# Four edits to an attention-plus-two-MLPs kernel: a weight's fetch behind stores, scores in shared banks, masks as two float32r parts, value means in place

## The chip, the cores and the metric

The kernel runs on one core of a Trainium2 chip. A run's time is the device time of one launch in microseconds (us). The time of a kernel is the median of its runs. TensorE is written PE here, VectorE DVE, ScalarE ACT, GpSimd POOL and SyncE SP; SP issues every transfer of this kernel.

## The reference

Three stages follow each other; all tensors are float32 except the six weight matrices, which are float64.

```python
# attention: batch 4, 8 heads, 768 tokens, head size 64; block 32, window 16
k_sum = k.reshape(B, H, nb, 32, D).max(axis=3)         # 24 block maxima of the keys
v_sum = v.reshape(B, H, nb, 32, D).mean(axis=3)        # 24 block means of the values
scores_l = where(|i - j| < 16, scale * q @ k.T, -1e9)  # local window
scores_s = scale * q @ k_sum.T + log(32)               # 24 summary columns
a = softmax(concat([scores_l, scores_s]))
x = a @ concat([v, v_sum])                             # 3072 tokens x 512
# first MLP, 512 -> 768 -> 512
h = maximum(maximum(x @ w1, x @ w2), x @ w3);  x = h @ w_out
# second MLP, 512 -> 2048 -> 512
h = x @ w_in;  out = (h * tanh(log1p(exp(h)))) @ w_out2
```

## The kernel before

**Number format.** A float32 matmul operand is written as a sum of two float32r parts, high and low, and a product is three float32r matmuls (high x high, high x low, low x high). A float32 operand can also be given to PE directly (`ident`, `mask`, the transposes).

**Attention** is done in 24 units of 128 tokens (6 for each batch). For unit `u`, `s2` multiplies queries with a window of 96 keys and 24 block maxima (`KX` = 120 columns) for 8 heads; the heads stand as 2 rows `r` of 4. The first three units (`u < PEMASK`) let PE add the mask: a matmul of the identity with the mask starts each bank (L435), and the scores are added to it. From the fourth unit on DVE adds the mask while it moves the scores out of PSUM (L452). DVE then finds the negative maximum (L455), ACT takes the exponentials (L459), `s2b` normalises, `s3` transposes the probabilities in two halves (`ptp`, L479, moved out as `pT` by ACT at L481), and `s4` multiplies with the values (`xp`, L493) and splits the result into high and low parts (`xh`, `xl`) for the first MLP. `q_prep` and `k_prep` transpose queries and keys (`tp`, L344); `k_prep` also takes the block maxima (`ksum`, L358) and stores transposed keys through the single buffer `kst` (L355, L360). `v_prep` takes block means of the values of batch 1 (`vp`, L298) and stores them through `vc`, which shares the buffer `kst` (L308 to L310).

**Weights.** A weight chunk is 128 rows x 512 float64 values (512 KB). `run_job` moves four chunks one step each through fetch (L159, three buffers `words`), absolute value on ACT (L169), five or six DVE instructions that make float32 out of float64 (L177 to L190) and a last step. For the first 24 chunks, those of the first MLP, the last step (`into`) leaves high and low parts in SBUF; the first 14 of them use PE to add up (`wp`, L232 to L234). For the 32 chunks of the second MLP (`later_jobs`, `keep`) the last step splits the chunk (L254, L255) and stores both parts to DRAM (`w2d`, L256 and L257), to be loaded later by `load_b`. A step is taken at each of the first units, and from token block 2 of the first MLP on once in three groups.

**First MLP.** Eight blocks of 384 tokens, each with 22 groups: 18 products of `gemm1` (`hp`, 12 matmuls, L584 to L586) and 4 of `gemm2` (`yp`, 18 matmuls, L618 to L620). ACT or DVE drains each result (L592, L596, L600, L622). Five steps of each attention unit are emitted between these groups. `y` goes to DRAM (L623).

**Second MLP.** Eight blocks of 384 tokens x 16 steps: `g3` (`up`, L677 to L679), an activation on ACT and DVE (L688 to L718), and `g4` into three accumulators (`acc`, L732 to L734).

[...] Before the change: pool `gps` has three one-bank buffers for `hp`, `yp`, `wp` and part of `up`; `aps` has three for `tp`, `vp`, `ptp` and `xp`; `asc` has one buffer of two banks for the scores `sc`. In the second MLP `aps` and `asc` are given back, and `ups` (two banks) and three accumulators take their place.

**Order.** The code above gives an order, and a scheduler that plans with its own model of the engines moves instructions within what data, buffers and `tc.issue_after` (this instruction comes after that one) allow. On the chip each engine then takes its instructions in that fixed order, so an instruction that waits holds up those behind it on its engine; that is also true of SP's transfers.

Of the kernel before, what the change touches and what calls it, by code (L numbers as in the profile page):

```python
# [10 lines left out]
F32 = mybir.dt.float32  # L11
# [3 lines left out]
ALU = mybir.AluOpType  # L15
# [38 lines left out]
def tile_kernel(ctx, tc, q, k, v, w1, w2, w3, w_out, w_in2, w_out2, out):  # L54
# [27 lines left out]
    dpool = ctx.enter_context(tc.tile_pool(name="dpool", bufs=1, space=DRAM))  # L82
    gps = ctx.enter_context(tc.tile_pool(name="gps", bufs=3, space=PSUM))

# [41 lines left out]
    g2 = agem.enter_context(tc.tile_pool(name="g2", bufs=1))  # L126

    att = ExitStack()
    ap1 = att.enter_context(tc.tile_pool(name="ap1", bufs=1, side="right"))
    ap2 = att.enter_context(tc.tile_pool(name="ap2", bufs=2, side="right"))  # L130
    ap3 = att.enter_context(tc.tile_pool(name="ap3", bufs=3, side="right"))
    stage = att.enter_context(tc.tile_pool(name="stage", bufs=WB, side="right"))
    aps = att.enter_context(tc.tile_pool(name="aps", bufs=3, space=PSUM))
    asc = att.enter_context(tc.tile_pool(name="asc", bufs=1, space=PSUM))

# [20 lines left out]
    def fetch(src):  # L156
        words = stage.tile([P, 1024], U32, name="words", tag="words")
        o, x = src(words)
        last["words"] = nc.sync.dma_start(out=o, in_=x)  # L159
        return words  # L160
# [90 lines left out]
    def keep(f, i):  # L251
        def done(w, _):
            h = stage.tile([P, 512], F32R, name="wr", tag="wr", bufs=AB)
            nc.scalar.copy(h, w)  # L254
            nc.vector.tensor_tensor(out=w, in0=w, in1=h.bitcast(F32), op=ALU.subtract)  # L255
            nc.sync.dma_start(out=w2d[f][:, 2 * i], in_=h.bitcast(F32))  # L256
            nc.sync.dma_start(out=w2d[f][:, 2 * i + 1], in_=w)  # L257

        return done
# [43 lines left out]
    def v_prep(b, g):  # L303

        t = nat.pop(("v", b, g))
        vp = aps.tile([P, H, D], F32, name="vp", tag="a")
        mean_v(vp[0:NS].rearrange("p h d -> p (h d)"), t, 0, NS, True, True)
        vc = ap1.tile([P, H, D], F32, name="vc", tag="kst")[0:NS]  # L308
        nc.scalar.copy(vc, vp[0:NS])
        nc.sync.dma_start(out=vsd[b][:, g * NS : (g + 1) * NS, :].rearrange("h n d -> n h d"), in_=vc)  # L310
# [59 lines left out]
    def q_prep(b, g):  # L370
        tp = turn("q", b, g)
        nc.scalar.mul(qT[(b * NG + g) % RQ], tp, scale)
# [43 lines left out]
    def bank(name):  # L416
        return aps.tile([P, NP, P], F32, name=name, tag="a")
# [9 lines left out]
    def s2(u):  # L427

        t = u % NG
        mask = masks["first" if t == 0 else "last" if t == NG - 1 else "mid"]  # L430
        sc = asc.tile([P, 2, 512], F32, name="sc", tag="sc")
        add = u >= PEMASK
        if not add:
            for r in range(2):
                nc.tensor.matmul(  # L435
                    sc[:, r, 0 : NP * KX], lhsT=ident, rhs=mask.unsqueeze(1).to_broadcast([P, NP, KX]),
                    start=True, stop=False,
                )
        for p in range(NP):
            for e in reversed(range(GT)):  # L440
                for r in range(2):
                    d = slice(r * D, (r + 1) * D)
                    c = slice(e * QT, (e + 1) * QT)
                    nc.tensor.matmul(
                        sc[c, r, p * KX : (p + 1) * KX], lhsT=qT[u % RQ][d, p, c], rhs=kT[(GT * u + e) % RK][d, p],
                        start=add, stop=add or p == NP - 1,
                    )
        s = ap2.tile([P, H, KX], F32, name="s", tag="s", bufs=SB)
        src = sc[:, :, 0 : NP * KX].rearrange("q r (p x) -> q r p x", p=NP)
        if add:  # L450
            wide = mask.unsqueeze(1).unsqueeze(1).to_broadcast([P, 2, NP, KX])
            nc.vector.tensor_tensor(out=heads(s), in0=src, in1=wide, op=ALU.add)  # L452
            src = heads(s)
        nm = ap2.tile([P, 2, NP], F32, name="nm", tag="nm")
        nc.vector.tensor_reduce(out=nm, in_=src, axis=AX.X, op=ALU.max, negate=True)  # L455
        sm = ap2.tile([P, H], F32, name="esum", tag="esum")
        for h in range(H):
            r, p = divmod(h, NP)
            nc.scalar.activation(  # L459
                out=s[:, h], in_=src[:, r, p], func=AF.Exp, bias=nm[:, r, p : p + 1], accum_out=sm[:, h : h + 1]  # L460
            )
        rs = ap2.tile([P, H, 1], F32, name="rs", tag="rs")
        att_t[u] = (s, sm, rs)
# [169 lines left out]
    def open_second():  # L633
# [5 lines left out]
        sec["t1"] = pool("bt1", 1)  # L639
        sec["up"] = sec["stack"].enter_context(tc.tile_pool(name="ups", bufs=2, space=PSUM))  # L640
        sec["ps"] = sec["stack"].enter_context(tc.tile_pool(name="bps", bufs=1, space=PSUM))
# [28 lines left out]
    def g3(i, f):  # L670
        xh, xl = x2hl[i]
        w = wb[f]
        more = (i * NF2 + f) % 5 > 2
        pt = (sec["up"] if more else gps).tile([P, 512], F32, name="up", tag="g")
        for c in range(KC):
# [85 lines left out]
    for T in range(RK):  # L761
        load_k(T)
    q_prep(0, 0)
    load_v(0)
    load_v(1)
    s2(0)
    run_job()
    s2b(0)
# [116 lines left out]
```

## Time and profile before

| | |
|---|---|
| median of 3 runs | 1132.24 us (1132.17 to 1132.39) |
| the profiled execution | 1133.17 us, of which the trace's span is 1131.4 us |
| busy in the span | PE 1098.0, DVE 812.4, ACT 549.6, POOL 75.8 us |
| mean granted PE clock | 0.994 of full speed |
| moved by DMA | 125.49 MB |
| second MLP | from about 540 us to the end |

A busy PE in this profile is not a PE at its peak: matmuls are pipelined, and their ends are modelled. In a row of the windows view the numbers are the stretch, its length, then for each engine busy us and instructions, the granted PE clock, the share of the DMA engines' time that was used and GB/s. In a row of the waits view they are who waited, for whom, us in total, times and the longest.

### The profile page before, as it was taken

The numbers are of one execution on the slowest core, as the hardware profiler recorded it, in microseconds if no ns is written. First come the engines' busy times: TensorE is split into PE (matmuls) and PEld (weight loads), VectorE is DVE, ScalarE is ACT, GpSimd is POOL, SyncE is SP. The second block draws the span as 40 slices with busy tenths as digits, with TensorE's granted clock in tenths as the row PEclk, the third lists the DMA queues.
The fourth block names the chain that finished last, engine by engine and source line by source line (L and its number), as shares of the span: only waits on it lengthen the run. The fifth ranks groups of instructions, "written<-read, shape, count | busy, mean of one in ns | idle before, by whom it ended". The sixth has DMA issues, their size and how long they took to land.

```text
span 1131.4 us, 18637 instructions
## 1 busy us (share of the span) xinstructions
PE 1098.0 (97%) x7004; PEld 987.8 (87%) x7004; DVE 812.4 (72%) x1595; ACT 549.6 (49%) x1336; POOL 75.8 (7%) x132
## 2 busy tenths in 40 slices
PE   6888999999999899999999999999999999999998
PEld 3557889999898899999999998989889898999887
DVE  5678934287887789852238887787878888787775
ACT  4676535345544554632125554545545455454543
POOL 3000012211113110100000000000000000000000
PEclk9999999999999899999999999999999999999999
DMA  9897745466887857521557010100001010000000
GB/s 234 217 253 201 174 126 135 125 172 197 225 215 221 228 172 201 159 68 52 179 189 288 15 57 1 55 2 23 35 1 56 1 29 29 14 29 1 29 1 28
DMA packets 179730, 125.49 MB, mean 111 GB/s; under 512 B 125048, under 2 KB 161400, under 8 KB 177592
## 3 DMA queue, kind: packets, MB, share of 16 engines
q1 hardware_dynamic: 179640, 124.30, 39.0%
q8 instruction: 55, 0.90, 0.3%
q14 instruction: 35, 0.29, 0.1%
HBM read 88.05 MB, written 35.05 MB: 109 GB/s over the span
## 4 chain that ended last, share of the span: by engine, by line
PE 77%; DVE 10%; ACT 5%; DMA 4%; issue 3%; POOL 1%; SPq 0%; ACTq 0%; POOLq 0%; DVEq 0%
PE up L679 8%; PE up L677 8%; PE acc L732 8%; PE up L678 8%; PE acc L733 8%; PE acc L734 8%; PE hp L584 6%; PE hp L586 6%; PE hp L585 6%; ACT s L459 3%; PE yp L618 2%; PE yp L620 2%; PE yp L619 2%; PE xp L493 1%; DVE words L182 1%
## 5 line engine op out<-in xcount | busy, mean ns | idle before, releaser
L695 ACT ACTIVATE r<-n,two 128x384 f32<-128x384 f32 x128 | 78.9, 616 | 153.9 <-DVE n L692 153.9
L584 PE MATMUL hp<-xh,a 128*128 128x384 f32 x384 | 133.9, 349 | 6.3 <-ACT m L592 3.4
L586 PE MATMUL hp<-xh,a 128*128 128x384 f32 x384 | 129.3, 337 | 0.0
L585 PE MATMUL hp<-xl,a 128*128 128x384 f32 x384 | 129.3, 337 | 0.0
L718 DVE TENSOR_TENSOR gl<-g,gh 128x384 fp32r<-128x384 f32 x128 | 71.3, 557 | 64.2 <-ACT gh L717 63.8
L688 ACT ACTIVATE e<-up 128x384 f32<-128x384 f32 x128 | 63.0, 492 | 98.8 <-PE up L679 97.9
L584 PEld LDWEIGHTS hp<-xh,a 128*128 128x128 f32 x384 | 72.4, 188 | 11.1 <-ACT m L592 4.3
L459 ACT ACTIVATE s<-s,nm 128x120 f32<-128x120 f32 x168 | 64.0, 383 | 29.5 <-DVE nm L455 29.5
L705 DVE TENSOR_TENSOR p<-up,r 128x384 f32<-128x384 f32 x128 | 70.6, 552 | 5.5 <-ACT r L696 5.5
L585 PEld LDWEIGHTS hp<-xl,a 128*128 128x128 f32 x384 | 72.5, 189 | 0.8 <-issue 0.5
L586 PEld LDWEIGHTS hp<-xh,a 128*128 128x128 f32 x384 | 72.4, 189 | 0.1
L690 DVE TENSOR_SCALAR ep<-e 128x384 f32<-128x384 f32 x128 | 45.9, 358 | 35.8 <-ACT e L688 35.3
L710 DVE SCALAR_TENSOR_TENSOR g<-u,n 128x384 f32<-128x384 f32 x128 | 70.9, 554 | 0.8
L708 DVE SCALAR_TENSOR_TENSOR u<-u,p 128x384 f32<-128x384 f32 x128 | 70.7, 552 | 0.4
L692 DVE SCALAR_TENSOR_TENSOR n<-e,ep 128x384 f32<-128x384 f32 x128 | 70.7, 552 | 0.3
L707 DVE SCALAR_TENSOR_TENSOR u<-n,r 128x384 f32<-128x384 f32 x128 | 70.3, 549 | 0.0
L717 ACT CAST gh<-g 128x384 fp32r<-128x384 f32 x128 | 64.3, 502 | 9.4 <-DVE g L710 9.4
L584 PE MATMUL hp<-xh,b 128*128 128x384 f32 x192 | 67.8, 353 | 0.3 <-ACT y L622 0.3
L696 ACT ACTIVATE r<-r 128x384 f32<-128x384 f32 x128 | 67.1, 524 | 1.0
L618 PE MATMUL yp<-hh,c 128*128 128x384 f32 x192 | 65.6, 344 | 0.1
L677 PE MATMUL up<-x2h,a 128*128 128x384 f32 x192 | 64.5, 336 | 0.0
L678 PE MATMUL up<-x2l,a 128*128 128x384 f32 x192 | 64.5, 336 | 0.0
(167 smaller groups left out, 2886.0 us busy)
## 6 DMA issues: line engine op xcount, KB each, us to landing
words<-in_moe_w_out SPq DMA_DIRECT2D x22, 512.0 KB, 4.7
words<-in_moe_w SPq DMA_DIRECT2D x18, 512.0 KB, 5.3
words<-in_moe_w_in SPq DMA_DIRECT2D x16, 512.0 KB, 3.9
w2d<-wr SPq DMA_DIRECT2D x32, 256.0 KB, 4.6
w2d<-wa SPq DMA_DIRECT2D x32, 256.0 KB, 5.2
kT<-kTd SPq DMA_DIRECT2D x35, 192.0 KB, 5.1
vr<-in_v SPq DMA_DIRECT2D x35, 192.0 KB, 3.6
nat<-in_q SPq DMA_DIRECT2D x24, 256.0 KB, 4.3
```

Of the source, the lines that this page charges most:

```text
L459: nc.scalar.activation(out=s[:, h], in_=src[:, r, p], func=AF.Exp, bias=nm[:, r, p : p + 1], accum_out=sm[:, h : h + 1])
L584: nc.tensor.matmul(pt[:, :n], lhsT=wh, rhs=xh[:, c, :n], start=(c == 0), stop=False)
L585: nc.tensor.matmul(pt[:, :n], lhsT=wh, rhs=xl[:, c, :n], start=False, stop=False)
L586: nc.tensor.matmul(pt[:, :n], lhsT=wl, rhs=xh[:, c, :n], start=False, stop=(c == KC - 1))
L618: nc.tensor.matmul(pt[:, :n], lhsT=wh, rhs=hh[:, :n], start=(f == 0), stop=False)
L677: nc.tensor.matmul(pt[:, :N2], lhsT=wh, rhs=xh[:, c], start=(c == 0), stop=False)
L678: nc.tensor.matmul(pt[:, :N2], lhsT=wh, rhs=xl[:, c], start=False, stop=False)
L679: nc.tensor.matmul(pt[:, :N2], lhsT=wl, rhs=xh[:, c], start=False, stop=(c == KC - 1))
L695: nc.scalar.activation(out=r, in_=d["n"], func=AF.Ln, bias=two[:, 0:1])
L732: nc.tensor.matmul(o, lhsT=gh[:, c], rhs=w[:, 2], start=(f == 0), stop=False)
L733: nc.tensor.matmul(o, lhsT=gh[:, c], rhs=w[:, 3], start=False, stop=False)
L734: nc.tensor.matmul(o, lhsT=gl[:, c], rhs=w[:, 2], start=False, stop=(f == NF2 - 1))
```

## The change

1. `fetch` issues a weight's fetch after the last store of the split weights (`last["store"]`), once there has been one. Nothing changes for the first 24 chunks.
2. The two-bank pool `asc` is gone. A unit's scores are two one-bank tiles, one for each row of heads, out of `aps`, which has four banks now. The free bank goes to `gps`, which has four. DVE's mask addition, and for the first three units its maximum, is done a row at a time. `ups` is gone; `up` lives in the four banks of `gps`.
3. The masks of the first three units are split into two float32r parts at the start (in the space of tiles `hh5`, `hl5`); PE adds them by two float32r matmuls a row in place of one float32 matmul.
4. `v_prep` writes the means over the tile that held the values (`t`), not to `kst`.

In the program's first lines `run_job` and `s2(0)` also come ahead of the loads of the first values.

```diff
-    gps = ctx.enter_context(tc.tile_pool(name="gps", bufs=3, space=PSUM))
+    gps = ctx.enter_context(tc.tile_pool(name="gps", bufs=4, space=PSUM))
...
+    split_masks = {}
+    for kind, tag in (("first", "hh5"), ("mid", "hl5")):
+        both = gx.tile([P, MAXT * QT], F32R, name=f"both_{kind}", tag=tag)
+        h, l = both[:, 0:KX], both[:, KX : 2 * KX]
+        nc.vector.tensor_copy(h, masks[kind])
+        nc.vector.tensor_tensor(out=l, in0=masks[kind], in1=h.bitcast(F32), op=ALU.subtract)
+        split_masks[kind] = h, l
...
-    aps = att.enter_context(tc.tile_pool(name="aps", bufs=3, space=PSUM))
-    asc = att.enter_context(tc.tile_pool(name="asc", bufs=1, space=PSUM))
+    aps = att.enter_context(tc.tile_pool(name="aps", bufs=4, space=PSUM))
...
-        last["words"] = nc.sync.dma_start(out=o, in_=x)
+        with tc.issue_after(last["store"].ins) if "store" in last else nullcontext():
+            last["words"] = nc.sync.dma_start(out=o, in_=x)
...
-            nc.sync.dma_start(out=w2d[f][:, 2 * i + 1], in_=w)
+            last["store"] = nc.sync.dma_start(out=w2d[f][:, 2 * i + 1], in_=w)
...
-        vc = ap1.tile([P, H, D], F32, name="vc", tag="kst")[0:NS]
+        vc = t[0:NS]
...
-        sc = asc.tile([P, 2, 512], F32, name="sc", tag="sc")
+        sc = [bank("sc") for r in range(2)]
...
-                nc.tensor.matmul(
-                    sc[:, r, 0 : NP * KX], lhsT=ident, rhs=mask.unsqueeze(1).to_broadcast([P, NP, KX]),
-                    start=True, stop=False,
-                )
+                for j, m in enumerate(split_masks[kind]):
+                    nc.tensor.matmul(
+                        sc[r][:, :, 0:KX], lhsT=one_r, rhs=m.unsqueeze(1).to_broadcast([P, NP, KX]),
+                        start=(j == 0), stop=False,
+                    )
...
-            wide = mask.unsqueeze(1).unsqueeze(1).to_broadcast([P, 2, NP, KX])
-            nc.vector.tensor_tensor(out=heads(s), in0=src, in1=wide, op=ALU.add)
+            for r in range(2):
+                wide = mask.unsqueeze(1).to_broadcast([P, NP, KX])
+                nc.vector.tensor_tensor(out=heads(s)[:, r], in0=src[r], in1=wide, op=ALU.add)
...
-        sec["up"] = sec["stack"].enter_context(tc.tile_pool(name="ups", bufs=2, space=PSUM))
...
-        more = (i * NF2 + f) % 5 > 2
-        pt = (sec["up"] if more else gps).tile([P, 512], F32, name="up", tag="g")
+        pt = gps.tile([P, 512], F32, name="up", tag="g")
...
+    run_job()
+    s2(0)
     load_v(0)
     load_v(1)
-    s2(0)
-    run_job()
```

The order that comes out of the scheduler moves in many places; two are shown. The first is PE near the program's start, from the second weight chunk's first matmul (`wp`) to the scores of the second unit. Before:

```order
L232 MATMUL wp<-words,ident 128x512
L435 MATMUL sc<-mask_mid,ident 128x480 x2
L233 MATMUL wp<-wr,one_r 128x512
L234 MATMUL wp<-a_343,neg_r 128x512
L344 MATMUL tp<-ident,nat 128x128 x4
L298 MATMUL vp<-vroom_204,mean 24x512 x4
L298 MATMUL vp<-vroom_205,mean 24x512 x2
L444 MATMUL sc<-kT_192,qT_188 64x120 x2
```

After, the same work (line numbers are those of the changed kernel):

```order
L240 MATMUL wp<-words,ident 128x512
L352 MATMUL tp<-ident,nat 128x128 x4
L306 MATMUL vp<-vroom_207,mean 24x512 x4
L306 MATMUL vp<-vroom_208,mean 24x512 x2
L445 MATMUL sc<-both_mid,one_r 128x4x120 x4
L241 MATMUL wp<-wr,one_r 128x512
L242 MATMUL wp<-a_350,neg_r 128x512
L454 MATMUL sc<-kT_195,qT_191 64x120 x2
```

The mask of the second unit has gone from ahead of the query transpose and the value means (`vp`) to behind both.

The second place is SP in the fourth block of the first MLP, where chunks of the second MLP's weights pass. Before:

```order
L159 DMA words<-in_moe_w_in 128x4x256
L623 DMA x2d_182<-y 128x384 x2
L318 DMA nat<-in_v 96x512 x2
L360 DMA kTd_174<-kst 512x1x128
L318 DMA nat<-in_v 96x512
L256 DMA w2d_161<-wr 128x512
L257 DMA w2d_161<-wa 128x512
L623 DMA x2d_182<-y 128x384
```

After:

```order
L326 DMA nat<-in_v 96x512
L638 DMA x2d_185<-y 128x384
L326 DMA nat<-in_v 96x512
L638 DMA x2d_185<-y 128x384
L326 DMA nat<-in_v 96x512
L368 DMA kTd_177<-kst 512x1x128
L264 DMA w2d_164<-wr 128x512
L265 DMA w2d_164<-wa 128x512
L167 DMA words<-in_moe_w_in 128x4x256
L638 DMA x2d_185<-y 128x384
```

The fetch (`words`) stood ahead of the first stores of `y`; it stands behind them and behind the two stores of split weights (`w2d`).

More of the change, by code (lines that the diff above doesn't have):

```diff
@@ L429, in s2 @@
         t = u % NG
-        mask = masks["first" if t == 0 else "last" if t == NG - 1 else "mid"]
-        sc = asc.tile([P, 2, 512], F32, name="sc", tag="sc")
+        kind = "first" if t == 0 else "last" if t == NG - 1 else "mid"
+        mask = masks[kind]
+        sc = [bank("sc") for r in range(2)]
         add = u >= PEMASK
@@ L444, in s2 @@
                     nc.tensor.matmul(
-                        sc[c, r, p * KX : (p + 1) * KX], lhsT=qT[u % RQ][d, p, c], rhs=kT[(GT * u + e) % RK][d, p],
+                        sc[r][c, p, 0:KX], lhsT=qT[u % RQ][d, p, c], rhs=kT[(GT * u + e) % RK][d, p],
                         start=add, stop=add or p == NP - 1,
@@ L448, in s2 @@
         s = ap2.tile([P, H, KX], F32, name="s", tag="s", bufs=SB)
-        src = sc[:, :, 0 : NP * KX].rearrange("q r (p x) -> q r p x", p=NP)
+        src = [x[:, :, 0:KX] for x in sc]
         if add:
-            wide = mask.unsqueeze(1).unsqueeze(1).to_broadcast([P, 2, NP, KX])
-            nc.vector.tensor_tensor(out=heads(s), in0=src, in1=wide, op=ALU.add)
-            src = heads(s)
+            for r in range(2):
+                wide = mask.unsqueeze(1).to_broadcast([P, NP, KX])
+                nc.vector.tensor_tensor(out=heads(s)[:, r], in0=src[r], in1=wide, op=ALU.add)
+            src = [heads(s)[:, r] for r in range(2)]
         nm = ap2.tile([P, 2, NP], F32, name="nm", tag="nm")
-        nc.vector.tensor_reduce(out=nm, in_=src, axis=AX.X, op=ALU.max, negate=True)
+        if add:
+            nc.vector.tensor_reduce(out=nm, in_=heads(s), axis=AX.X, op=ALU.max, negate=True)
+        else:
+            for r in range(2):
+                nc.vector.tensor_reduce(out=nm[:, r], in_=src[r], axis=AX.X, op=ALU.max, negate=True)
         sm = ap2.tile([P, H], F32, name="esum", tag="esum")
@@ L459, in s2 @@
             nc.scalar.activation(
-                out=s[:, h], in_=src[:, r, p], func=AF.Exp, bias=nm[:, r, p : p + 1], accum_out=sm[:, h : h + 1]
+                out=s[:, h], in_=src[r][:, p], func=AF.Exp, bias=nm[:, r, p : p + 1], accum_out=sm[:, h : h + 1]
             )
```

## Prediction

> **What bounds the kernel now.** I read the page's first part for the engines' shares, then the windows of 30 us to see which engine is full where.
>
> ```profile
> span 1131.4 us, 18637 instructions
> PE 1098.0 (97%) x7004; PEld 987.8 (87%) x7004; DVE 812.4 (72%) x1595; ACT 549.6 (49%) x1336; POOL 75.8 (7%) x132
> ```
>
> ```profile
> 0.00:30.00 30.00, 20.38 (x87) 10.41 (x88) 15.20 (x27) 14.44 (x36) 10.91 (x51) 0.94 0.94 236
> 30.00:60.00 30.00, 24.75 (x236) 14.23 (x234) 21.50 (x39) 20.91 (x60) 1.72 (x3) 1.00 0.91 221
> 60.00:90.00 30.00, 26.65 (x217) 18.46 (x218) 22.52 (x42) 20.86 (x60) 0.00 (x0) 0.94 1.04 246
> 90.00:120.00 30.00, 27.00 (x214) 24.13 (x210) 29.12 (x58) 17.25 (x42) 1.13 (x4) 1.00 0.70 181
> 150.00:180.00 30.00, 30.00 (x215) 28.12 (x214) 9.37 (x16) 10.95 (x32) 5.37 (x7) 1.00 0.42 105
> 360.00:390.00 30.00, 27.12 (x240) 24.30 (x239) 24.14 (x44) 12.28 (x34) 6.24 (x11) 0.89 0.81 218
> 600.00:630.00 30.00, 30.00 (x153) 27.13 (x152) 24.84 (x54) 15.04 (x31) 0.00 (x0) 1.00 0.68 275
> ```
>
> PE is idle for 1131.4 - 1098.0 = 33.4 us in all. From 0 to 90 it has 30 - 20.38 + 30 - 24.75 + 30 - 26.65 = 18.2 us of that, and there the DMA engines are nearly full (shares 0.94, 0.91, 1.04): weights and first inputs come in. From 90 to 120 DVE is full (29.12 of 30), converting weights. From 150 on PE is full, but for a stretch in the middle (27.12 of 30 from 360 to 390, with the clock at 0.89). The second MLP, from 600 as in every later window, leaves PE no gap; nothing in the change shortens PE's work there. So a gain can come from two places: the start, and the waits in the middle. The waits view of PE says what these are:
>
> ```profile
> PE hp L584 <- ACT m L592: 3.4, 4, 2.2
> PE hp L584 <- DVE m L596: 2.3, 2, 1.9
> PE tp L344 <- ACT vc L309: 1.2, 1, 1.2
> ```
>
> The first two are products that wait for a bank of `gps` that ACT or DVE has not drained. The clock around the longest of them, in windows of 3 us (length, PE busy, clock, DMA share, GB/s):
>
> ```profile
> 379.00:382.00 3.00, 1.55 (x10) 0.84 0.62 146
> 382.00:385.00 3.00, 3.00 (x36) 0.50 0.82 288
> 385.00:388.00 3.00, 3.00 (x36) 0.53 0.80 184
> ```
>
> Right behind the wait PE runs at half its clock. That loses 3 x (0.16 + 0.50 + 0.47) = 3.4 us of PE's work.
>
> **The start: masks and the order of the first units.** The chain of waits runs through PE here:
>
> ```profile
> 22.88 3.43 PE sc L435 x4
> 26.77 0.44 PE tp L344 x4
> 27.21 5.26 PE vp L298 x12
> 34.48 0.90 PE wp L232 x2
> 35.38 0.23 PE wp L233
> 37.25 5.26 DMA words<-in_moe_w
> ```
>
> The second unit's mask starts only at 22.88, when ACT has read the first unit's scores out of the one `sc` buffer; it takes 3.43, partly at a low clock. Behind it stand the query transpose, the value means, and at 34.48 the third chunk's widening matmul, which frees a `words` buffer; only then is the next weight fetched. Meanwhile nothing is transferred:
>
> ```profile
> 32.00:34.00 2.00, 2.00 (x40) 1.00 0.02 5
> 34.00:36.00 2.00, 2.00 (x12) 1.00 0.00 0
> ```
>
> The changed order has the transpose and the means ahead of the mask, and the scores have other banks, so PE need not stand until 22.88. What is late next is the query tile:
>
> ```profile
> 17.77 0.85 SPq L295 DMA_DIRECT2D nat<-in_q  x1
> nat<-in_q SPq DMA_DIRECT2D x24, 256.0 KB, 4.3
> ```
>
> It lands at about 17.77 + 0.85 + 4.3 = 22.9. The new mask: a float32 matmul of 512 columns takes 0.90 (L232), a float32r one 0.23 (L233), so two of 480 columns for each of two rows take 4 x 0.23 x 480/512 = 0.86, against 2 x 0.90 x 480/512 = 1.69 at the same clock for the old one. From the transpose to the widening, the path is then 0.44, the 34.48 - 27.21 = 7.27 from the means through scores, transpose and half the probabilities, the mask's 0.86, and chunk two's two matmuls, 0.46: 22.9 + 9.0 = 31.9 instead of 34.48, **2.5 us** earlier. Behind it the DMA engines are full until about 90, so what is gained here is carried on by DMA, then by DVE, then by PE. The bounds are 0, if the transfers end no sooner, and 4.0, the whole pause of the two rows above. I take 2.5, since each term has a row. The first unit's mask moves behind the key transposes; its cover is the wait for the keys, and four small DVE instructions that split the masks lie where DVE has no work yet. Both at nothing.
>
> **The stage that DVE bounds.** With the means written in place, `vc` no longer waits for the store of `kst`, and the 1.2 us of PE's wait goes (bounds 0 and 1.2; the value tile is held until its store has landed, so a load into it may come later, beside other loads). Against it stand DVE's split additions:
>
> ```profile
> L452 DVE TENSOR_TENSOR s<-sc,mask_mid x14: 1148/1149/1158, 58.9 to 469.9; 128x960 f32<-128x960 f32 x14
> 379.23 0.55 DVE L596 TENSOR_TENSOR m<-hp,m 128x384 f32<-128x384 f32 x1
> ```
>
> On the line between 384 elements at 0.55 and 960 at 1.15, 480 take 0.65: a unit pays 2 x 0.65 - 1.15 = 0.15 more. Of 21 units three lie where DVE bounds: 0.45. Elsewhere PE's work covers it. Together **0.75 us** gained.
>
> **The middle: a fourth bank for products.** One more bank lets PE go on for one more product before it needs the drain:
>
> ```profile
> 353.67 0.44 PE L584 MATMUL hp<-xh,b 128*128 128x384 f32 x1 [0.29 <-ACT y L622]
> 355.69 0.34 PE L586 MATMUL hp<-xh,b 128*128 128x384 f32 x1
> ```
>
> Twelve starts in 2.02 us, so a product is 2.2 us, and no wait of the two rows is longer than 2.2. All **5.7 us** (3.4 + 2.3) can go, and with them the half clock: **3.4 us**. What makes the drains late is in part the fetch, here at SP, in order of issue:
>
> ```profile
> SPq L159 <- DVE wa L190: 45.6, 18, 5.1
> 343.83 0.39 SPq L159 DMA_DIRECT2D words<-in_moe_w_in  x1
> 344.46 0.80 SPq L623 DMA_DIRECT2D x2d<-y  x2
> ```
>
> SP stood at the fetch until DVE had freed its buffer, and the stores of `y`, for whose buffer ACT waits, stood behind it. The new order lets these past. The added wait puts the fetch behind both stores of a chunk; whatever follows it on SP had to wait for it anyway. A fetch that is 2 us later harms nobody, as fetch and first reader of one chunk show:
>
> ```profile
> 357.38 0.33 SPq L159 DMA_DIRECT2D words<-in_moe_w_out  x1
> 373.94 0.67 ACT L169 ACTIVATE wa<-words 128x512 f32<-128x512 f32 x1
> words<-in_moe_w_out SPq DMA_DIRECT2D x22, 512.0 KB, 4.7
> ```
>
> Of 16.6 us the transfer needs 4.7. So I cost the fetch's move at nothing, and its gain is inside the 5.7. Bounds for both terms: 0 and 9.1.
>
> **The banks' price.** In `aps` six tiles a unit now turn through four banks, so the second half of a unit's probabilities, and the third transpose where keys are prepared, get the bank of the next unit's first scores: PE stands until DVE has added the mask. Worst seen is this unit:
>
> ```profile
> 366.16 1.05 PE L444 MATMUL sc<-kT,qT 64*64 64x120 f32 x32
> 374.99 1.15 DVE L452 TENSOR_TENSOR s<-sc,mask_last 128x960 f32<-128x960 f32 x1
> ```
>
> Its scores are ready at 367.2, and the first half would be added at 374.99 + 0.65 = 375.6. The changed order has 24 product matmuls and a query transpose between, 24 x 2.2/12 + 0.44 = 4.8 us, so PE would stand 3.6. At most of the other units DVE is less late. Bounds 0 and 3.6 for this one; I take **2.0** lost, since what made DVE late is partly removed.
>
> **The sum.** 2.5 + 0.75 + 5.7 + 3.4 - 2.0 = 10.35 us. The profiled execution, 1133.17, becomes 1122.8; it lies 0.93 above the median, 1132.24, which becomes **1121.9**. `up` in four banks instead of five costs nothing: ACT and DVE have read a bank within about two steps, of four that it may be held.
>
> **The rivals.**
> - *The clock still halves.* The windows' rows tie the drop to PE's gaps, the longest 1.9 us in the waits view, with 1.45 of 3 us idle. If it has another cause, 3.4 us stay lost: 1125.3. For it: the drop is one event. [...] Chance 0.14.
> - *The start is not earned.* The full DMA engines end their work when they did: 1121.9 + 2.5 = 1124.4. Against: 4 us of empty engines. Chance 0.12.
> - *The middle's waits come back elsewhere*, since DVE still converts the same chunks and ACT, in order, waits for it: 9.1 us stay, and the loss of 2.0 falls away as part of them, so 2.5 + 0.75 = 3.25 remain: 1129.0. For it: DVE at 24.14 of 30. Chance 0.15.
> - *Slower: the scores' banks hold PE up.* The place is the unit whose scores end at 74.41 and whose addition starts at 88.63:
>
> ```profile
> 73.36 1.05 PE L444 MATMUL sc<-kT,qT 64*64 64x120 f32 x32
> 88.63 1.16 DVE L452 TENSOR_TENSOR s<-sc,mask_last 128x960 f32<-128x960 f32 x1 [1.00 <-PE ptp L479]
> ```
>
> If the next tiles need that bank, PE stands until 89.3, 14.9 us; with 3.6 at the other place 18.5, less the gains of 12.35: 1138.4. It decides once such waits pass 12.35 us. Against: in the new order product matmuls follow most scores, and here DVE's last wait was for PE itself (`ptp`, which empties a tile `s`), so a PE that comes sooner shortens it. Chance 0.10.
>
> The forecast has the rest, 0.49.
>
> **How the numbers follow.** Low end: the whole pause (1.5 more), no loss to banks (2.0), all of `vc` (0.45), and some 2 us of the start's other waits: 1116. High end: the start, the clock and part of the middle not earned: 1130, which holds all but the slower rival and the worst of the third. About 0.2% (2.3 us) is what a measurement can tell from no change. Faster by more: the forecast 0.49, the first two rivals 0.26, three quarters of the third 0.11: 0.86. The rest of the third, 0.04, is within; slower 0.10.
>
> **What would show it.** Right: the windows of 30 us from 0 to 60 hold more PE work and no empty DMA; in the waits view `hp` on ACT and DVE is under 1 us; no half clock after 150; SP's waits at the fetch nearly gone. Wrong: new waits of `ptp`, `xp` or `tp` on DVE's mask addition of several us, a longer second MLP, or ACT waiting for `words`.

## The result, and the profile after

The changed kernel takes 1120.41 us (median of 4 runs, 1118.76 to 1122.32); the kernel before, run again beside it, 1132.20. The ratio is 0.9904 with a 95% interval of 0.9877 to 0.9932. In a second set of runs on one chip with the experiments below the ratio was 0.9895 (0.9876 to 0.9914), 1119.89 us. The profiled execution took 1121.29 us, its span is 1119.5. So it is faster by about 11 us, near the forecast of 1121.9. The profile says that it got there by another way than the sum.

The page's first part, and the windows of 30 us of the changed kernel (length, then busy time of PE, PE's weight loads, DVE, ACT and POOL, then clock, DMA share and GB/s):

```profile
span 1119.5 us, 18658 instructions
PE 1087.2 (97%) x7004; PEld 986.9 (88%) x7004; DVE 816.1 (73%) x1623; ACT 548.6 (49%) x1336; POOL 77.4 (7%) x132
```

```profile
0.00:30.00 30.00, 18.97 (x82) 10.53 (x83) 16.31 (x31) 14.19 (x35) 10.50 (x51) 0.89 0.96 239
30.00:60.00 30.00, 24.12 (x242) 15.17 (x240) 21.58 (x39) 19.63 (x58) 2.18 (x3) 1.00 0.83 210
60.00:90.00 30.00, 27.02 (x168) 18.91 (x169) 24.72 (x48) 23.83 (x66) 0.00 (x0) 0.89 1.09 240
90.00:120.00 30.00, 30.00 (x281) 27.49 (x280) 28.90 (x56) 18.09 (x52) 1.72 (x4) 1.00 0.85 208
150.00:180.00 30.00, 27.11 (x172) 25.88 (x173) 9.73 (x18) 11.02 (x33) 3.29 (x4) 0.94 0.41 108
360.00:390.00 30.00, 28.27 (x220) 27.03 (x220) 23.38 (x44) 15.52 (x51) 6.46 (x8) 1.00 0.84 207
```

Up to 60 us PE does less than before (18.97 and 24.12 against 20.38 and 24.75), and the clock of the first 30 us has fallen from 0.94 to 0.89. From 90 to 120 PE, which had 27.00, is full. A gap with half clock behind it (0.50 from 158.02 to 161.43) is new from 150 to 180, where before was full. From 360 to 390 the clock is back at 1.00. Some of PE's waits, in the whole span (who waited for whom at which line, then us in total, times, and the longest):

```profile
PE wp L240 <- DVE words L190: 7.9, 2, 5.9
PE hp L599 <- ACT y L637: 2.0, 1, 2.0
PE yp L633 <- ACT hh L618: 1.9, 2, 1.3
PE yp L633 <- ACT c L235: 1.5, 2, 0.9
PE ptp L494 <- DVE s L463: 1.5, 1, 1.5
```

The waits of `hp` for `m` are gone, on ACT and on DVE. In their place stand smaller ones, among them `ptp` on DVE's mask addition, the banks' price. Two larger rows of the first 70 us are left out here: `xp` on its own issue (5.6, before 2.0) and the first transposes on the loads of the keys (4.9). The wait for `words` has the same total as before, but one of its pieces, at the start, is now 5.9 us long; before there were five, none above 1.9:

```profile
PE wp L232 <- DVE words L182: 7.9, 5, 1.9
```

To see where the 11.9 us between the two profiled executions lie, I read from PE's timeline when the first product of a block starts. Block 4 of the first MLP starts at 281.8 before and at 280.9 now: 0.9 us. Blocks 4 and 5 together take 138.8 before and 129.2 now: **9.6 us**. From there to the last `up` matmul it is 697.2 and 695.9: 1.3. (These, and the times in the table below, are differences of rounded times, good to 0.1.) So nearly all of the gain lies between 281 and 410 us, and the start gave almost nothing.

**The start.** PE's timeline of the changed kernel (start, length, the instructions, and in brackets the idle time ahead of them and what ended it):

```profile
12.02 1.95 PE L445 MATMUL sc<-both_first,one_r 128*128 128x480 f32 x4
22.71 2.07 PE L240 MATMUL wp<-words,ident 128*128 128x512 f32 x2 [5.86 <-DVE words L190]
24.58 1.05 PE L352 MATMUL tp<-ident,nat 128*128 128x128 f32 x4
25.56 6.68 PE L306 MATMUL vp<-vroom,mean 128*24 128x512 f32 x12
32.17 1.15 PE L445 MATMUL sc<-both_mid,one_r 128*128 128x480 f32 x4
35.62 1.07 PE L240 MATMUL wp<-words,ident 128*128 128x512 f32 x2
```

The new mask is about as short as worked out (1.15 us for the second unit, the last matmul's whole length in it). But the second chunk's widening matmul stands ahead of the query transpose and the value means in PE's order, as the order listed under "The change" has it, and PE waits 5.86 us for DVE's `words`. What DVE works on comes from ACT, and ACT's timeline shows why it is late:

```profile
16.65 0.36 ACT L474 ACTIVATE s<-sc,nm 128x120 f32<-128x120 f32 x1 [1.08 <-DVE nm L470]
19.35 0.69 ACT L177 ACTIVATE wa<-words 128x512 f32<-128x512 f32 x1
```

In the new order ACT has the eight exponentials of the first unit, from 16.65 on, ahead of the second chunk's absolute value at 19.35, which was at 18.1 before. So the widening starts at 22.71; before it started at 21.51. Behind the gap the transposes and a part of the means run at half clock (0.50 from 21.48 to 28.31), and the mask, now behind the means, ends at 33.3. The third chunk's widening, the end of the path that the sum had worked out, starts at 35.62. Before it was 34.31 in the same view (34.48 in the row that the prediction shows), and the sum had it at 31.9. The transfers pause as before: from 32 to 38 us the DMA share in windows of 2 us is 0.04, 0.00 and 0.07.

**The queue of SP.** The waits of SP's queue before, in the whole span, for the fetch (L159, beside the 45.6 shown in the prediction), the first store of a weight chunk (L256) and the stores of `y` (L623):

```profile
SPq L623 <- ACT y L622: 42.1, 15, 6.5
SPq L159 <- DVE wa L177: 39.7, 6, 11.5
SPq L256 <- ACT wr L254: 11.9, 19, 2.7
```

And after, for the fetch (L167), the first store of a weight chunk (L264) and the stores of `y` (L638):

```profile
SPq L264 <- ACT wr L262: 78.7, 25, 10.7
SPq L638 <- ACT y L637: 42.6, 16, 6.0
SPq L167 <- DVE wa L198: 8.7, 4, 3.4
```

SP does not stand much less: most of what it waited at the fetch it now waits at the store ahead of it.

### The profile page after: what moved, and what is told of

Read it like the earlier page. It is cut to its first block, busy times and chain, and to the rows that moved or that the text cites. A ratio compares the mean times of both kernels' runs of the same rounds, so it can differ in the third digit from the quotient of the medians.

```text
span 1119.5 us, 18658 instructions
## 1 busy us (share of the span) xinstructions
PE 1087.2 (97%) x7004; PEld 986.9 (88%) x7004; DVE 816.1 (73%) x1623; ACT 548.6 (49%) x1336; POOL 77.4 (7%) x132
## 4 chain that ended last, share of the span: by engine, by line
PE 75%; DVE 11%; ACT 6%; DMA 4%; issue 2%; SPq 1%; POOL 1%; ACTq 0%; POOLq 0%; DVEq 0%
PE up L692 8%; PE up L690 8%; PE acc L745 8%; PE up L691 8%; PE acc L746 8%; PE acc L747 8%; PE hp L599 5%; PE hp L600 5%; PE hp L601 5%; ACT s L474 3%; PE yp L633 2%; PE yp L634 2%; PE yp L635 2%; DMA kT<-kTd 1%; DVE words L190 1%
## 5 line engine op out<-in xcount | busy, mean ns | idle before, releaser
L600 PE MATMUL hp<-xl,a 128*128 128x384 f32 x384 | 129.5, 337 | 0.0
L601 PE MATMUL hp<-xh,a 128*128 128x384 f32 x384 | 129.3, 337 | 0.0
L611 DVE TENSOR_TENSOR m<-hp,m 128x384 f32<-128x384 f32 x48 | 26.5, 553 | 53.4 <-PE hp L601 48.7
```

Source lines behind the costliest of these rows:

```text
L600: nc.tensor.matmul(pt[:, :n], lhsT=wh, rhs=xl[:, c, :n], start=False, stop=False)
L601: nc.tensor.matmul(pt[:, :n], lhsT=wl, rhs=xh[:, c, :n], start=False, stop=(c == KC - 1))
```

## The experiments

Each kernel below was timed in five rounds beside the kernel before. The table has every one: median, ratio to before with its interval, when DVE starts its last instruction on a weight chunk of the first MLP (the last `c` in the first 200 us), when block 4 starts, how long blocks 4 and 5 take, and the rest up to the last `up` matmul, all of the profiled execution. The medians are of many executions; the last four columns are of one each.

| kernel | us | ratio (95%) | last `c` | block 4 starts | blocks 4+5 | rest |
|---|---|---|---|---|---|---|
| before | 1130.6 to 1132.2 | 1 | 148.2 | 281.8 | 138.8 | 697.2 |
| changed | 1120.4 | 0.9904 (0.9877 to 0.9932) | 151.9 | 280.9 | 129.2 | 695.9 |
| changed, again | 1119.9 | 0.9895 (0.9876 to 0.9914) | 151.9 | 281.1 | 128.8 | 695.9 |
| changed, three banks | 1122.9 | 0.9933 (0.9921 to 0.9945) | 151.5 | 280.6 | 129.4 | 696.8 |
| changed, free fetch | 1126.7 | 0.9956 (0.9941 to 0.9970) | 153.4 | 280.7 | 134.9 | 696.3 |
| changed, means ahead of widening | 1116.9 | 0.9875 (0.9861 to 0.9889) | 149.5 | 278.8 | 130.1 | 695.8 |
| changed, `vc` in its own tile | 1118.6 | 0.9906 (0.9886 to 0.9926) | 151.5 | 277.9 | 129.5 | 695.9 |
| before + banks | 1123.0 | 0.9932 (0.9920 to 0.9945) | 145.9 | 275.7 | 133.7 | 697.2 |
| before + shared scores alone | 1127.3 | 0.9972 (0.9960 to 0.9985) | 150.0 | 282.5 | 132.6 | 698.9 |
| before + fetch | 1128.1 | 0.9982 (0.9966 to 0.9998) | 148.5 | 282.6 | 133.1 | 697.4 |
| before + masks | 1129.6 | 0.9986 (0.9973 to 1.0000) | 151.1 | 278.8 | 137.3 | 697.2 |
| before + means | 1125.2 | 0.9947 (0.9932 to 0.9963) | 146.4 | 278.9 | 138.5 | 697.2 |
| banks + fetch | 1115.8 | 0.9871 (0.9853 to 0.9889) | 145.2 | 276.0 | 128.6 | 695.8 |
| banks + fetch, means ahead of widening | 1122.0 | 0.9915 (0.9893 to 0.9936) | 159.4 | 286.0 | 129.3 | 695.8 |

Two theories were to be told apart. Theory A: the banks, above all the fourth one for products, carry the gain in the middle, as predicted. Rival B: the fetch's place carries it, which the sum had at nothing. Beside them stood theory C on the start: the widening ahead of the means is what lost it.

### The changed kernel with three product banks

```diff
-    gps = ctx.enter_context(tc.tile_pool(name="gps", bufs=4, space=PSUM))
+    gps = ctx.enter_context(tc.tile_pool(name="gps", bufs=3, space=PSUM))
-        pt = gps.tile([P, 512], F32, name="up", tag="g")
+        more = (i * NF2 + f) % 5 > 2
+        pt = (sec["up"] if more else gps).tile([P, 512], F32, name="up", tag="g")
```

> The changed kernel with one edit undone: products have three banks again, and the second MLP's `up` its two more; the scores stay in the four shared banks. Theory A (the fourth product bank carries the gain in the middle): the waits of `hp` for `m` on ACT and DVE come back, 4 to 6 us in all, with a stretch of half clock behind the longest, and the time rises by 5 to 9 us, to 1125.5 to 1129.5. Rival B (the waits went because the stores no longer stand behind the fetch on SP, or because units come earlier): `hp` on `m` stays under 1.5 us and the time is 1119.5 to 1121.5.

Measured: 1122.9, between the two. Blocks 4 and 5 take 129.4, much as with four banks (129.2 and 128.8). PE's waits in that stretch (280 to 411 us; the line is the only one there on `m`):

```profile
PE hp L599 <- ACT m L607: 1.6, 1, 1.6
```

So the 5.3 us of waits that before has there do not come back with the third bank; 1.6 does (2.4 in the whole span), and no half clock (the mean clock from 280 to 411 is 1.00). Theory A falls for the middle. The fourth bank is still worth some 3 us in all, 0.9933 against 0.9895 and 0.9904. Where they lie the traces don't show: these three differ by no more than 1 us in any of the columns.

### The changed kernel with a free fetch

```diff
-        with tc.issue_after(last["store"].ins) if "store" in last else nullcontext():
-            last["words"] = nc.sync.dma_start(out=o, in_=x)
+        last["words"] = nc.sync.dma_start(out=o, in_=x)
```

> The changed kernel with one edit undone: the fetch of a chunk no longer waits for the stores of the chunk ahead. Theory A (the banks carry the gain): SP's wait at the fetch comes back (some 40 to 50 us), but nobody waits for SP, and the time is within 1 us, 1119.4 to 1121.4. Rival B (the fetch's place carries it): ACT and PE wait for y's buffer again in the middle, and the time rises by 3 to 6 us, to 1123.5 to 1126.5.

Measured: 1126.7, with blocks 4 and 5 at 134.9, 5.7 us more than in the changed kernel. That is 0.2 us above rival B's range; "within 1 us" fell. SP's waits at the fetch are back, as in before:

```profile
SPq L166 <- DVE wa L197: 54.1, 23, 5.6
SPq L166 <- DVE wa L184: 38.5, 6, 11.3
```

So is ACT's wait for `y`'s buffer, which the store of `y` must first have emptied. In blocks 4 and 5 of this kernel, and of the changed one:

```profile
ACT y L636 <- DMA x2d<-y: 7.7, 3, 3.1
```

```profile
ACT y L637 <- DMA x2d<-y: 1.1, 2, 0.6
```

### The kernel before with banks alone, with the fetch alone, with shared scores alone

The first has the pools and `s2` of the changed kernel, with the old masks, means and fetch:

```diff
-    aps = att.enter_context(tc.tile_pool(name="aps", bufs=3, space=PSUM))
-    asc = att.enter_context(tc.tile_pool(name="asc", bufs=1, space=PSUM))
+    aps = att.enter_context(tc.tile_pool(name="aps", bufs=4, space=PSUM))
-        sc = asc.tile([P, 2, 512], F32, name="sc", tag="sc")
+        sc = [bank("sc") for r in range(2)]
```

The third is the first with `gps` at 3 and `ups` restored. The second has only this:

```diff
-        last["words"] = nc.sync.dma_start(out=o, in_=x)
+        with tc.issue_after(last["store"].ins) if "store" in last else nullcontext():
+            last["words"] = nc.sync.dma_start(out=o, in_=x)
```

> The kernel before with one edit alone: scores in two of four shared banks, a fourth bank for products, `up` in these four; masks in float32 by one matmul a row, the fetch free, the means through their own tile. Theory A (the banks carry the gain in the middle): the waits of `hp` for `m` fall below 1 us, scores stand in one piece, and the time falls by 5 to 9 us, to 1123 to 1127. Rival B (the fetch's place or the masks carry it): 1 to 3 us at most, 1129 to 1131.

> The kernel before with one edit alone: the fetch of a chunk behind the stores of the chunk ahead. Theory F (in the fourth and fifth blocks of the first MLP, where before takes 138.8 us and the changed kernel 129.2, the fetch's place carries about half of the gain): these two blocks take 133 to 135.5 us and the time falls by 3 to 6 us, to 1125 to 1128. Theory A (the banks carry all of it): 138 to 139 us, and a time within 1.5 us of before.

> The kernel before with half of one edit: scores in two of four banks shared with the other tiles, but three banks for products and two more for `up`, as before; masks, fetch and means as before. Theory F (the sharing carries the other half, the fourth product bank nothing): the time is within 1.5 us of that with both halves (1123.0), 1121.5 to 1124.5. Theory A as predicted (the fourth product bank carries it): `hp` waits for `m` again 4 to 6 us, and the time is 1127 to 1131.

Measured in blocks 4 and 5: 133.7, 133.1 and 132.6, against 138.8. Each of sharing and fetch, by itself, brings 5.7 to 6.2 of the 9.6 us there. The fourteen traces fall into four groups by these two edits, whatever else is in the kernel: with neither 137.3 to 138.8 (three traces), with the fetch alone 133.1 (one), with the sharing alone 132.6 to 134.9 (three), with both 128.6 to 130.1 (seven). So the fetch is worth 5.1 to 5.7 whatever stands beside it, and the sharing 5.1 to 6.2 on the kernel before and 4.5 beside the fetch (133.1 to 128.6).

What the 5.7 and the 6.2 are made of: PE is idle in these blocks for 6.3 us before, for 3.4 with the fetch alone and for 4.7 with the shared scores alone; and the stretch at half clock, which costs 3.4, is in before (0.50 from 381.02 to 387.85) and in neither of the two (mean clock 1.00 from 282 to 416).

The fourth bank on top of the sharing shows no gain there (133.7 against 132.6). But of these two traces the first has a stretch at half clock, 3.4 us (mean clock 0.97 from 275 to 410), and the second none (1.00 from 282 to 416), so a gain of 2 us may be hidden. PE's waits in these blocks: before (281 to 421 us), then the fetch alone (282 to 416), the shared scores alone (282 to 416) and both halves of the banks (275 to 410):

```profile
PE hp L584 <- ACT m L592: 3.0, 3, 2.2
PE hp L584 <- DVE m L596: 2.3, 2, 1.9
```

```profile
PE hp L585 <- DVE m L597: 1.5, 1, 1.5
PE hp L585 <- ACT m L593: 1.2, 2, 0.6
```

```profile
PE hp L589 <- ACT m L597: 3.2, 3, 1.6
PE ptp L484 <- DVE s L453: 1.1, 1, 1.1
```

```profile
PE ptp L484 <- DVE s L453: 2.3, 1, 2.3
PE ptp L484 <- DVE xl L508: 0.7, 1, 0.7
PE hp L589 <- ACT m L597: 0.3, 1, 0.3
```

The fetch by itself halves the waits of `hp`, from 5.3 to 2.7. The sharing by itself takes them to 3.2, with 1.1 new at `ptp`. The fourth bank on top of the sharing then does what was said of it, 3.2 become 0.3, but `ptp` stands 3.0 instead of 1.1: with the fetch free, most of the wait for a bank has only changed its name. With sharing, fourth bank and fetch together `ptp` is at 1.5 and `hp` at none. ACT's wait for `y`'s buffer, before and with the fetch alone, falls here too:

```profile
ACT y L622 <- DMA x2d<-y: 9.3, 3, 3.8
```

```profile
ACT y L623 <- DMA x2d<-y: 4.7, 3, 3.3
```

In time the fourth bank does help, 1127.3 to 1123.0. In the traces most of that lies in the first 282 us, where block 4 starts at 275.7 instead of 282.5; but one is of its kernel's slowest execution (1129.3) and the other of the fastest (1121.9), so they show more than the 4.3 between the medians. Theory A's range for the banks alone, 1123 to 1127, was met at its lower edge. For the shared scores alone F's 1121.5 to 1124.5 was a miss. A's 1127 to 1131 was met there, and its 4 to 6 us of `hp` on `m` too: 4.7 in the whole span, of which 3.2 lie in these blocks. The fetch alone met F's 133 to 135.5 for the two blocks and missed its 1125 to 1128 by less than 0.1. It is worth 4.8 us between the two profiled executions (1133.2 and 1128.4), of which 5.7 lie in blocks 4 and 5, and 2 to 3 us between the medians: a part of it is not there in every run.

### The start: the widening behind the means, the masks, the means

Theory C's kernel issues the second chunk's widening matmuls behind the last matmul of the value means:

```diff
+            means = last.pop("means", None)
+            with tc.issue_after(means.ins) if means else nullcontext():
+                nc.tensor.matmul(sums, lhsT=ident, rhs=w, start=True, stop=False)
```

> The changed kernel with one thing moved: on TensorE the widening matmuls of the second weight chunk stand behind the value means instead of ahead of them. Theory C (the start was lost because TensorE stood 5.9 us at that widening, in order, with the query transpose and the value means ready behind it): that wait goes from 5.9 to under 1.5 us, the half clock at 21 to 28 us goes, the first product of the first block comes at 67.5 to 69 instead of 71.7, and the time falls by 2 to 4 us, to 1116.5 to 1118.5. Rival D (the transfers and DVE's conversions bound the first 150 us whatever TensorE does): the first product comes earlier or not, but the second block still starts at 156.5 to 157.5, and the time is 1119.5 to 1121.5.

Measured: 1116.9, in C's range, and its reason fell all the same. (The interval, 0.9861 to 0.9889, overlaps the changed kernel's two, so that even the gain of 3 us is not quite certain.) The wait for `words` went to 0.5, but PE then stood for the query tile; in the whole span of this kernel:

```profile
PE tp L354 <- DMA nat<-in_q: 7.0, 1, 7.0
PE wp L242 <- DVE words L190: 0.8, 2, 0.5
```

The first product of the first block came at 75.7, not at 67.5 to 69. To see whether the place of the widening is worth anything, the same edit was made on the fastest kernel, that with banks and fetch alone:

> The changed kernel with two edits undone: masks again in float32, value means again through their own tile. Banks and fetch stay. Theory F: the fourth and fifth blocks take 129 to 130 us as in the changed kernel, 4 us less than with the banks alone; if the second block then starts at 150 to 151 us, as with the banks alone (150.1), and not at 157.2, masks or means had cost the start some 7 us, and the time is 1114 to 1118. Rival G (the early second block with the banks alone came from the free fetch): the second block starts at 156 to 158 and the time is 1119 to 1122.

> The kernel with banks and fetch alone, and the second chunk's widening behind the value means as well. Theory M (the start is bound by the transfers and by DVE's conversions; whatever TensorE waits for there only moves; what counted in the changed kernel with this move was that the last chunks came earlier): within 1.5 us of banks and fetch alone (1115.8), 1114.3 to 1117.3, and the PE's loss up to 70 us stays at 38 to 43. Theory C (the widening's place is itself worth 2 to 4 us): 1112 to 1114.

Banks and fetch alone take 1115.8, all four runs (1114.3 to 1117.8) below all of the changed kernel's (1118.7 to 1122.3). Blocks 4 and 5 take 128.6, the second block starts at 150.4: theory F held. With the widening moved as well it takes 1122.0. The same edit, three matmuls moved behind twelve, seems to take some 3 us off one kernel and adds 5 to 6 to the other; C and M both missed. What moved with the time is the last conversion on DVE. The rows of `c` in the first 200 us (count, ns of one, first and last start) of before, changed, banks and fetch, and the same with the widening moved:

```profile
L229 DVE TENSOR_TENSOR c<-wa,c x6: 679/682/693, 119.4 to 148.2; 128x512 fp32r<-128x512 f32 x6
```

```profile
L237 DVE TENSOR_TENSOR c<-wa,c x6: 680/684/1935, 122.0 to 151.9; 128x512 fp32r<-128x512 f32 x6
```

```profile
L229 DVE TENSOR_TENSOR c<-wa,c x6: 676/692/2173, 122.8 to 145.2; 128x512 fp32r<-128x512 f32 x6
```

```profile
L229 DVE TENSOR_TENSOR c<-wa,c x6: 684/693/707, 133.1 to 159.4; 128x512 fp32r<-128x512 f32 x6
```

And what PE waits for between 100 and 170 us, in banks and fetch, and with the widening moved:

```profile
PE yp L624 <- ACT c L227: 0.8, 1, 0.8
```

```profile
PE yp L626 <- ACT c L227: 3.5, 2, 3.2
```

In the table, among the kernels with the old masks, block 4 starts later where the last `c` is later: 145.2 and 145.9 with 276.0 and 275.7, then 146.4 with 278.9, 148.2 and 148.5 with 281.8 and 282.6, 150.0 with 282.5, 159.4 with 286.0. Those with the split masks, whose PE work is shorter at the start (2.6 us by the expectation's estimate), lie 2 to 5 us below. It is a tendency and no line: from 145.9 to 146.4 block 4 moves by 3.2 us, from 150.0 to 159.4 by 3.5, and with the split masks 151.5 goes with 280.6 and with 277.9. DVE is nearly full there (29.12 of 30 us before, from 90 to 120); what may decide is how many units' additions, maxima and products its order has ahead of the last chunk. The order is worked out anew for every kernel, so a small edit at 15 us can change it at 120. That the last conversion sets the start is argued from these fourteen traces; no experiment moved it alone.

The remaining two edits, alone on the kernel before, and the means undone in the changed one:

```diff
-                nc.tensor.matmul(
-                    sc[:, r, 0 : NP * KX], lhsT=ident, rhs=mask.unsqueeze(1).to_broadcast([P, NP, KX]),
-                    start=True, stop=False,
-                )
+                for j, m in enumerate(split_masks[kind]):
+                    nc.tensor.matmul(
+                        sc[:, r, 0 : NP * KX], lhsT=one_r, rhs=m.unsqueeze(1).to_broadcast([P, NP, KX]),
+                        start=(j == 0), stop=False,
+                    )
...
-        vc = ap1.tile([P, H, D], F32, name="vc", tag="kst")[0:NS]
+        vc = t[0:NS]
```

> The kernel before with one edit alone: the masks as two float32r parts. Theory M (TensorE's saving of some 2.6 us in three units lies under the waits of the start, and the changed order lets one more unit's work stand ahead of the last weight chunks on DVE): the absolute value of the 24th chunk comes later than before's 137.2, at 140 to 145, and the time is between before's and 3 us above it, 1130.5 to 1134. Rival (the shorter masks are a gain, as predicted): the 24th chunk comes by 137 and the time is 1.5 to 3 us below before's, 1127.5 to 1129.

> The kernel before with one edit alone: the value means written in place. As predicted: TensorE's wait of 1.2 us for `vc` goes, and the time falls by up to 1.2 us, to 1129.4 to 1130.6. Rival (the value tile, held until its store has landed, delays later loads): 0.5 to 3 us above before, 1131 to 1134.

> The changed kernel with one edit undone: the value means go through their own tile again. Theory H (written in place they hold the value tile until their store has landed, and so delay the first block's loads): the second block starts at 150 to 153 us instead of 157.2, and the time is 1114 to 1118. Rival (the means' place is worth the 1.2 us that was predicted, or nothing): the second block starts at 156.5 to 158.5, and the time is 1119.5 to 1122.

The masks alone: 1129.6, between both expectations and hardly to be told from before (the interval reaches 1.0000), with the 24th chunk at 141.3 and the last `c` 2.9 us later than before, as M has it. On top of banks and fetch they cost some 3 to 4 us: 1115.8 and 0.9871 without them, 1118.6 and 0.9906 with them, both with the old means; the intervals just overlap. The means alone are worth 6.0 us, far over the 1.2 us, and a miss of both expectations; in the changed kernel they are worth nothing (0.9906 without, 0.9895 and 0.9904 with). There the second block starts at 155.5 and the time is 1118.6; both lie between theory H's ranges and the rival's, so both missed. The cause of the 6 us is open: the profiled execution of that kernel, 1129.9, was the slowest of nine (from 1124.6), and shows 2.9 us of them by block 4.

The last run is the changed kernel once more, for comparison on the same chip:

> The changed kernel itself once more, beside these on one chip, so that they are compared with it and not only with before. Its ratio to before was 0.9904 (0.9877 to 0.9932): 0.989 to 0.992 again, 1118.5 to 1122.

1119.9, and the same marks as in the first trace to 0.4 us.

## Why the prediction was right, and where its steps were wrong

**The forecast held as a number** because two errors cancel, which is luck. The sum had 3.25 us from the start and 7.1 us from the middle; the traces have 0.9 and 9.6, and 1.3 behind.

**The start, 2.5 us, was not earned.** The step that failed is "what is late next is the query tile". Late next was the second chunk's `words`, and PE's order had its widening ahead of the transpose. The order that stands under "The change" shows this: its first row is that widening. The path's end, the third chunk's widening, came at 35.62 and not at 31.9. The rival "the start is not earned" came true, and its reason, that the DMA engines end their work when they did, is left open: what the traces show first is that PE stood behind a conversion. The move of the widening showed that the wait then goes on to the query tile, 7.0 us, until 24.54 and not 22.9 as worked out. The order of the calls at the start does nothing by itself: with the calls as before and all else changed, every engine has the same instructions in the same order.

**The masks' 0.86 us was about right in size** (1.15 with the last matmul's whole length) and brought no time that the runs could tell from none: alone 0.9986 (0.9973 to 1.0000). That PE waits for weights there anyway is argued.

**The DVE stage, 0.75 us.** The wait for `vc` went, as said. What seems to matter in that stage is not the 0.45 for three split additions but when DVE comes to the last chunk: 148.2 before, 151.9 after, 145.2 without the split masks and the new means.

**The fourth bank, 5.7 us: right in size, wrong in its cause.** The waits went to none. But with three banks, and the fetch moved, blocks 4 and 5 are as fast to 0.6 us. The sharing of the score banks, which the sum had only as a price, and the fetch, which it had at nothing, each by itself take 2.1 and 2.6 of the 5.3 us of waits there, and the half clock with them. In all the fourth bank is worth 3 to 4 us between the medians, at places that the traces don't settle. That `up` has four banks instead of five costs nothing, as said: with five the rest takes 696.8, with four 695.9.

**The fetch at nothing was the largest mistake of the sum.** In blocks 4 and 5 it brings 5.7 us alone, 5.7 on top of the other edits, and 5.1 on top of the banks. (Between the medians it is 2 to 3 us alone and 6 to 7 on top of the others or of the banks.) The step that failed is "its gain is inside the 5.7": the slack of 16.6 us against a landing of 4.7 says that a later fetch harms nobody, and that was so; what it does not say is what the stores behind a standing SP were worth. The prediction names them, and that ACT waits for them; their price shows in ACT's wait for `y`'s buffer, 9.3 us before and 4.7 with the fetch alone, 7.7 with the free fetch and 1.1 in the changed kernel.

**The half clock, 3.4 us, came as said.** The mean clock from 280 to 411 is 1.00 in the changed kernel. With the banks alone the half clock returned: 0.89 from 360 to 390, the 30 us in which that kernel's `ptp` wait of 2.3 lies. There it costs about 30 x 0.11 = 3.3 us, as in the same 30 us of before (0.89). With three banks, the fetch alone and the shared scores alone the mean clock of these blocks is 1.00. So it stood once behind waits of `hp` and once in the 30 us of one of `ptp`. In the changed kernel a gap of 2.0 at 155 us has half clock behind it (0.50 from 158.02 to 161.43), in a stretch that before had none.

**The banks' price, 2.0 us:** 1.5 measured, at the unit that was named. The slower rival, 14.9 us behind the unit at 74 us, did not come: the view of waits has no `ptp`, `xp` or `tp` on DVE's addition but the one of 1.5. Of the rival by which the middle's waits come back elsewhere a part is true: `ptp` 1.5, `yp` on `hh` 1.3 in these blocks, and `hp` on `y` 2.0 at 155 us.

What the terms leave of the 9.6 us is 9.6 - 5.3 (`hp`) - 3.4 (clock) + 1.5 (`ptp`) + 1.3 (`yp` on `hh`) = 3.7. In these blocks the scores begin nine times before and six times after: a unit's scores now come in one piece, not split among products. Whether a switch costs PE anything was not shown by itself, and it can't be all: with the shared scores alone they begin six times too, and PE's busy time less the loss of the half clock is 128.0 there, against 129.1 before and 126.1 in the changed kernel. What the rest is stays open.

## What to carry to other kernels

Where one queue issues loads, stores and fetches in order, cost a wait by what stands behind it in the queue, not by whether the waiting transfer has slack: here ACT's wait for `y`'s buffer was 9.3 us in the middle before and 4.7 with the fetch moved. Where several edits may cure the same wait, don't give the whole of it to one: here the fetch's place and the sharing of banks each brought 5 to 6 us in the middle, and the fourth bank, to which the sum gave it all, little there that can be seen. And read a forecast's first row against the order that the kernel will run: the start was lost to an instruction that the listing had on top. PE's waits at the start move from one row to the next when one is taken away (5.9 us for `words` became 7.0 for the query tile), so an edit's gain there must be measured in the kernel in which it will stand: the best of these kernels has two of the four edits.

## What the runs showed of the hardware

The clock that PE was granted is on record from 12.38 us of before's trace on and from 14.66 us of the changed kernel's. It is 1.00 or 0.50 there, and within each of the two traces all recorded changes lie whole multiples of 3.41 us apart. Up to 1100 us it is 0.50 in three stretches of each:

| trace | clock 0.50 | PE idle in the 3.41 us ahead |
|---|---|---|
| before | 22.62 to 26.03 | 1.86 |
| before | 60.17 to 63.58 | 1.88 |
| before | 381.02 to 387.85 | 1.87 |
| changed | 21.48 to 28.31 | 3.41 |
| changed | 62.44 to 69.27 | 2.06 |
| changed | 158.02 to 161.43 | 2.02 |

Other stretches of 3.41 us with much idle time have a clock of 1.00 behind them: 49.93 to 53.34 of before (1.65 idle) and 48.79 to 52.20 of the changed kernel (1.73), and 1125.13 to 1128.54 of before (1.79), where PE's work ends. Three stretches with the ones behind them, of the changed kernel, of the free fetch (1.72 idle, then 1.00) and of the shared scores alone (1.80 idle, then 0.50):

```profile
154.59:158.00 3.41, 1.39 (x8) 1.06 (x7) 0.38 (x2) 3.41 (x16) 0.55 (x1) 1.00 1.28 254
158.00:161.41 3.41, 3.41 (x13) 3.41 (x12) 0.69 (x1) 2.05 (x5) 2.69 (x4) 0.50 0.67 232
```

```profile
155.09:158.50 3.41, 1.69 (x13) 1.36 (x11) 0.75 (x3) 3.22 (x17) 0.00 (x0) 1.00 1.23 277
158.50:161.91 3.41, 3.08 (x18) 3.08 (x19) 0.93 (x3) 2.43 (x6) 2.41 (x2) 1.00 0.97 281
```

```profile
69.11:72.52 3.41, 1.61 (x15) 0.77 (x16) 2.39 (x5) 3.41 (x8) 0.00 (x0) 1.00 1.11 305
72.52:75.93 3.41, 3.41 (x59) 2.99 (x56) 2.97 (x6) 2.32 (x5) 0.00 (x0) 0.50 1.14 297
```

No run changed PE's idle time alone, so what sets the clock was not shown. As an estimate from these rows, 3.41 us at 0.50 cost up to 3.41 x 0.50 = 1.7 us; whether that is why runs of one kernel differ by 3 to 5 us here was not shown either.
